# Sinkhorn attention and a Sinkhorn-routed mixture on one core: the last sums of expert 0's first weights are put behind VectorE's sums of x, and a weight fetch in front of them

## The chip, the core and the metric

The kernel runs on one core of a Trainium2 chip. The metric is the device time of one execution, in microseconds (us). The core has five engines with queues of their own, which meet only through semaphores: TensorE (PE, matrix multiply; its weight loads are listed as PEld), VectorE (DVE), ScalarE (ACT), GpSimd (POOL) and SyncE (SP, here only for transfers). Matmuls write to PSUM, which is used here as 8 banks of 128 x 512 float32; everything else lies in SBUF. Transfers run beside the engines, but each is issued by an instruction on the queue of SP, ACT or POOL.

## The reference

Two stages in a row: block-sorted attention, whose output is the x of a mixture of experts with Sinkhorn-balanced gates.

```python
# attention: batch 4, heads 8, sequence 768, head size 64, 8 blocks of 96
P = sort_net                                   # 8 x 8 for each batch and head
for _ in range(5):                             # exp, then rows and columns to sum 1
    P = np.exp(P - P.max(-1, keepdims=True))
    P = P / (P.sum(-1, keepdims=True) + 1e-09)
    P = P / (P.sum(-2, keepdims=True) + 1e-09)
k_sorted = einsum('bhij,bhjcd->bhicd', P, k_b) # blocks of k and v mixed by P
v_sorted = einsum('bhij,bhjcd->bhicd', P, v_b)
attn = softmax(scale * q_b @ k_sorted.T)       # within each block
x = (attn @ v_sorted) as 3072 tokens x 512
# mixture: 8 experts, 512 -> 1024 -> 512
P = np.exp(x @ w_gate - max)
for _ in range(8):                             # rows, columns, times N / E
    P /= P.sum(1, keepdims=True) + 1e-09; P /= P.sum(0, keepdims=True) + 1e-09; P *= N / E
for e in range(8):
    out += P[:, e:e+1] * (np.maximum(x @ w1[e], 0) @ w2[e])
```

## The kernel before

**Two parts.** The first part goes through the four batches of attention. While batch bb is at work, PE also gets pieces of expert 0's dense work on the tokens of batch bb - 1 (`expert0`), so that it has something to do while ACT and DVE prepare the next scores. The second part works off the rest of expert 0 (tokens 2048 to 3071) and experts 1 to 7, with seven block products in place of eight (a Strassen-like scheme): it needs sums and differences of blocks of w1 (`sum_w`), of x (`sum_x`), of w2 (`sum_w2`) and of the hidden layer.

**Who sets the order.** `pin` keeps an instruction at its place in the written order of its engine; what is not pinned is placed by a scheduler. All work of PE and POOL in the stretch concerned is pinned but for one memset; the first `sum_x` on DVE is not. Attention of batch bb follows a string, `PLANS[bb]`: q, k, s, d, m are queries, keys, scores, sums and mixing for a pair of heads, a number n takes n pieces of expert 0's work, g and l are gate logits, L loads the next batch, v sorts values. W and w in `PLANS[3]` take 9 and 2 sums from `w1_sums`, a chain of `sum_w(1)` and `sum_w(0)`, eight sums for each expert, all on POOL (L323). `load_next(3)` took five before. So of the sixteen, five come with the load, nine at W (the last three of expert 1 and six of expert 0), two at w. For expert 0 the two that overwrite blocks of w1 itself come last (`late`).

**PSUM in the first part.** Scores, sums, mixing and expert 0 share a ring of 8 banks (pool `pa`): a matmul into a bank waits until the bank's reader of eight allocations ago is done. The matmuls of L221 (scores) are 16 for a pair of heads, into four banks, eight matmuls for two banks at a time. The matmuls of L408 fill a bank with an output tile of expert 0, which L413 copies to SBUF on DVE or ACT. L395 is the hidden layer of expert 0, L262 mixes the values, L265 scales the result into `xtT` (x transposed) on DVE, L253 and L254 on ACT form the reciprocal of the softmax sums that L244 has formed.

**Around the seam.** After attention `load_w2(1)` fetches expert 1's w2 into a new pool, on POOL's queue (L95). `onesc` is a memset on POOL (L556). `sum_x(0, nc.vector, ...)` makes four sums on DVE (L552), over the first of three token ranges: three into `xc`, one that overwrites a block of `xtT`. `xs` is `sum_x(2, nc.vector)`, the third range; `sum_x(1, nc.gpsimd)` is the second, on POOL. `held_x` is a copy of two columns of `xc` (L807) that keeps POOL waiting for the third of `xs`'s sums; behind it stand the eight sums of w2 (L542). The sums of expert 0's w1 lie in `osbl`, in tiles that the output doesn't need yet; PE reads them at L611.

```python
    3: "1 g q0,q1,k0,k1,k2 3 q2,q3,s0 W 4 k3,d0,s1 4 m0,d1,s2 6 m1,d2,s3 4 w 1 m2,d3 2 m3 1"
    ...
    w1_sums = in_turn(sum_w(1), sum_w(0))
    ...
    for a, b, c in ((b12, b11, x1), (b22, x1, x2), (b21, x2, x4), (b22, b12, b12)):
        hold(eng.tensor_tensor(out=c, in0=a, in1=b, op=ALU.subtract))
```

Of the kernel before, what the change touches and what calls it, by code (L numbers as in the profile page):

```python
# [15 lines left out]
BF16 = mybir.dt.bfloat16  # L16
# [10 lines left out]
def kernel(  # L27
# [11 lines left out]
    nc = tc.nc  # L39
# [20 lines left out]
    pin = tc.keep_in_program_order  # L60
# [3 lines left out]
    xtT = xtp.tile([128, 4, N], BF16)  # L64
# [79 lines left out]
    def sort_values(bb, bank, n=8, h0=0):  # L144
        for h in range(h0, n):
            vps = bank([128, 384], F32)
            pin(nc.tensor.matmul(vps, Rt[bb][:, h].rearrange("p i c -> p (i c)"),  # L147
                                 vt[bb][:, h, :], start=True, stop=True))
            (nc.vector.tensor_copy if bb == 0 and h in (3, 5, 7) or bb and h % 2 else
             nc.scalar.copy)(  # L150
                vs[:, :, h, :], vps.rearrange("p (kk d) -> p kk d", d=64))
            if h % 2:
                yield

        for i in (0, 1, 2, 3, 4, 6, 5, 7) if bb == 0 else range(NB if n == 8 else 0):
            eng = ((nc.scalar if i == 1 else nc.gpsimd if i in (5, 7) else nc.sync)
                   if bb == 0 else nc.gpsimd if i % 2 and bb == 1 else nc.sync)
            if bb == 0 and i == 5:
                yield
            (pin if bb == 0 else lambda ins: ins)(eng.dma_start(  # L160
                out=mkap(vsbt[bb % 2], [[VW, 96], [1, 512]], off=i * 512),
                in_=vs[16 * i:16 * i + 16].rearrange("p kk h d -> p kk (h d)")))
# [3 lines left out]
    def queries(bb, hp, bank):  # L166

        qps = bank([128, 6, 128], BF16)
        if bb < 2:

            for kk in range(6):
                for h in range(2):
                    pin(nc.tensor.matmul(qps[64 * h:64 * h + 64, kk, :],
                                         qt[bb][:, 2 * hp + h, kk * 64:kk * 64 + 64],
                                         Ibig, is_transpose=True, start=True, stop=True))
        else:
            qr = sp.tile([128, 6, 2, 64], BF16, name="qr", bufs=2)
            nc.gpsimd.tensor_copy(
                qr.rearrange("p kk h d -> p h kk d"),
                qt[bb][:, 2 * hp:2 * hp + 2].rearrange("p h (kk d) -> p h kk d", d=64))  # L180
            for kk in range(6):
                pin(nc.tensor.matmul(qps[:, kk, :], qr[:, kk].rearrange("p h d -> p (h d)"),  # L182
                                     Ibig, is_transpose=True, start=True, stop=True))
        qT[bb, hp] = sp.tile([128, 128, 6], BF16, name="qTs", bufs=4)
        (pin if bb == 0 else lambda ins: ins)(
            (nc.scalar.copy if bb == 0 or hp < 2 or bb == 1 else nc.vector.tensor_copy)(
                qT[bb, hp], qps.rearrange("p kk c -> p c kk")))

    def keys(bb, hp, bank):

        kT[bb, hp] = sp.tile([128, NB, 16, 6], BF16, name="kTs", bufs=4)
        for b in range(2):
            kps = bank([128, 3, 128], F32)
            for j in range(3):
                kk = 3 * b + j
                for h in range(2):
                    pin(nc.tensor.matmul(  # L197
                        kps[64 * h:64 * h + 64, j, :],
                        kt[bb][:, 2 * hp + h, kk * 64:kk * 64 + 64],
                        Rt[bb][:, 2 * hp + h].rearrange("p i c -> p (i c)"),  # L200
                        start=True, stop=True))
            (order if bb == 0 else lambda ins: ins)(
                (nc.scalar.copy if (bb, hp, b) in ((0, 0, 1), (0, 1, 0)) else nc.vector.tensor_copy)(
                    kT[bb, hp][:, :, :, 3 * b:3 * b + 3],
                    kps.rearrange("p kk (i c) -> p i c kk", i=8)))
# [65 lines left out]
    def logits(bb, bank, ks):  # L271

        if 0 in ks:
            gp[bb] = bank([128, TB, E], F32)
        for kk in ks:
            for t in range(TB):
                c = bb * S + t * 128
                pin(nc.tensor.matmul(gp[bb][:, t, :], xtT[:, kk, c:c + 128], wg[:, kk],
                                     start=(kk == 0 and t == 0), stop=(kk == 3),
                                     skip_group_check=True))  # L280
        if 3 in ks:
            nc.vector.tensor_copy(glog[:, bb * TB:(bb + 1) * TB, :], gp[bb])

    def first_attention(bank, warm, fill):
# [9 lines left out]
        for x in PLAN0.split():  # L294
# [8 lines left out]

    wct = {}

    def sum_w(e):

        if e:
            wct[e] = (wcq if e % 2 == 0 else wcp).tile([128, 3, 2, F // 2], BF16, name="wc")
        else:  # L310
            wct[e] = osbl[:, NT - 3:].rearrange("p t d -> p (t d)").bitcast(BF16).rearrange(
                "p (j k f) -> p j k f", j=3, k=2)
        late = []
        for kk in range(2):
            a11, a21 = (w1t[e][:, kk, f:f + 512] for f in (0, 512))
            a12, a22 = (w1t[e][:, 2 + kk, f:f + 512] for f in (0, 512))
            s1, s2, s4 = (wct[e][:, j, kk, :] for j in range(3))
            todo = [(a21, a22, ALU.add, s1), (s1, a11, ALU.subtract, s2),
                    (a11, a21, ALU.subtract, a21), (a12, s2, ALU.subtract, s4)]
            if e == 0:  # L320
                late.append(todo.pop(2))
            for a, b, o, c in todo + (late if e == 0 and kk else []):
                pin(nc.gpsimd.tensor_tensor(out=c, in0=a, in1=b, op=o))  # L323
                yield
# [11 lines left out]
    w1_sums = in_turn(sum_w(1), sum_w(0))  # L336

    def attention(bb, bank, fill):

        def sorts():  # L340
            for b in {1: (1, 2), 2: (3,), 3: ()}[bb]:
                yield from sort_values(b, bank)
                yield

        values = sorts()

        def step(what, hp):
            if what == "q":
                queries(bb, hp, bank)
            elif what == "k":  # L350
                keys(bb, hp, bank)
            elif what == "s":
                scores(bb, hp, bank)
            elif what == "l":
                logits(bb, bank, (0, 1, 2))
            else:
                for b in range(2):
                    (sums if what == "d" else mix)(bb, hp, b, bank)

        for x in PLANS[bb].split():  # L360
            if x == "v":
                next(values)
            elif x == "g":
                logits(bb - 1, bank, (0, 1, 2, 3))
            elif x == "L":
                load_next(bb + 1)
            elif x in "Ww":
                for _ in range(9 if x == "W" else 2):
                    next(w1_sums)
            elif x.isdigit():  # L370
                for _ in range(int(x)):
                    next(fill)
            else:
                for y in x.split(","):
                    step(y[0], int(y[1]))
# [132 lines left out]
    mpc, xcp, wq, wcq = late("mpc", 1), late("xcp", 1), late("wq", 2), late("wcq", 1)  # L508
# [36 lines left out]
    xc = xcp.tile([128, 3, 2, N // 2], BF16)  # L545

    def sum_x(p, eng, hold=pin):
        ta, tb = (slice(1024 * p + 512 * i, 1024 * p + 512 * i + 512) for i in range(2))
        b11, b12, b21, b22 = (xtT[:, k:k + 2, t] for k in (0, 2) for t in (ta, tb))
        x1, x2, x4 = (xc[:, j, :, 512 * p:512 * p + 512] for j in range(3))  # L550
        for a, b, c in ((b12, b11, x1), (b22, x1, x2), (b21, x2, x4), (b22, b12, b12)):
            hold(eng.tensor_tensor(out=c, in0=a, in1=b, op=ALU.subtract))  # L552
            yield

    onesc = mpc.tile([128, 128], F32)
    nc.gpsimd.memset(onesc, 1.0)  # L556
    for _ in sum_x(0, nc.vector, lambda ins: ins):
        pass

    def balance():  # L560
# [230 lines left out]
    for i in (0, 2):  # L791
        take = iter(six[i]).__next__
        two = [hidden(0, 2, i + j, hTb[1], None, False, take)[0] for j in range(2)]
        for n, step in enumerate([f for both in zip(*two) for f in both]):
# [8 lines left out]
            if (i, n) == (0, 5):  # L803
                for _ in xs:
                    pass
    held_x = mpc.tile([128, 2], BF16)
    pin(nc.gpsimd.tensor_copy(held_x, xc[:, 2, 0, 1024:1026]))  # L807

    queue = [sum_w2(1), sum_x(1, nc.gpsimd)]

# [13 lines left out]
    for m, o in enumerate(ends):  # L824
        e, p, hT, _ = chunks[-1]
# [4 lines left out]
    for r in range(len(pairs) + 6):  # L830
        n, i = r // 4, r % 4
        if n < C:
            e, p, hT, s3 = chunks[n]
# [83 lines left out]
```

## Time and profile before

| | |
|---|---|
| Runs before, median (lowest to highest of 3) | 662.59 us (662.49 to 663.95) |
| The profiled execution, whole | 662.44 us |
| Its span in the profile | 660.7 us |
| Granted clock of PE over the span | 1.0 |
| Chain that ended last, share of PE | 95% |
| Of it L611 and L724, the second part's matmuls | 40% and 38% |
| POOL's wait for expert 1's w2 and two later ones, L542 (3 times) | 15.5 us |
| POOL's wait for PE's L395, at L323 | 8.5 us |
| POOL's wait for DVE's sum of x, at L807 | 3.5 us |

Times in a timeline are counted from the start of the span. In such a row the first number is the start, the second the duration, and brackets hold how long the engine sat idle before it, and what ended that. Where a row says x2 or more, the duration covers all of them. The profiled execution has the instructions' durations; it is one of the kernel's runs, and its own time stands beside its span so that sums over rows are made against it.

### The profile page before, as it was taken

To read this page: it belongs to the slowest core of one execution; us is meant where nothing else is said; L and a number is where in the kernel's file an instruction comes from. 1 tells how busy PE (TensorE), PEld (TensorE's weight loads), DVE (VectorE), ACT (ScalarE), POOL (GpSimd) and SP (SyncE) were. 2 spreads that over 40 slices of the span, in tenths; PEclk is the share of its full clock that TensorE was granted. 3 is DMA by queue.
4 is the path that set the end of the run, shared out by engine and by line. 5 is a ranking of instruction groups with operands and counts; after the bars stand their busy time and mean duration, and the time that the engine had idled before them with its cause. 6 is when DMAs were issued, how large, how long until landed. Compare 5 with 4: busy or idle time off the path is not lost.

```text
span 660.7 us, 13144 instructions
## 1 busy us (share of the span) xinstructions
PE 647.5 (98%) x5035; PEld 422.0 (64%) x5035; DVE 476.2 (72%) x897; ACT 390.1 (59%) x765; POOL 476.2 (72%) x438
## 2 busy tenths in 40 slices
PE   5999998999999999999999999999999999999997
PEld 2556665445666666666666666666666666666665
DVE  6857587666777777777777777777777777777775
ACT  5877766757777755555555555555555555555540
POOL 3543564477999898689696969799796969946641
PEclk9999999999999999999999999999999999999999
DMA  9999930406103040211303040302103040000224
GB/s 150 183 222 143 204 64 1 65 1 97 32 1 64 2 65 1 44 22 15 50 1 65 1 65 1 65 1 38 27 3 63 1 64 2 1 1 34 95 80 176
DMA packets 34031, 36.52 MB, mean 55 GB/s; under 512 B 2352, under 2 KB 27376, under 8 KB 33968
## 3 DMA queue, kind: packets, MB, share of 16 engines
q0 software_dynamic: 26448, 26.81, 26.1%
q1 hardware_dynamic: 7120, 8.38, 4.4%
q8 instruction: 39, 0.64, 0.4%
q10 hardware_dynamic: 400, 0.49, 0.2%
q14 instruction: 24, 0.20, 0.1%
HBM read 52.45 MB, written 6.29 MB: 89 GB/s over the span
## 4 chain that ended last, share of the span: by engine, by line
PE 95%; DMA 2%; DVE 1%; issue 1%; POOL 1%; DVEq 0%; POOLq 0%
PE bk L611 40%; PE oacc L724 38%; PE bank L395 4%; PE bank L408 4%; PE oacc L778 2%; DMA kt<-in_k_dram 2%; PE bank L221 1%; PE bk L690 1%; PE bank L262 1%; PE bank L244 1%; PE bank L197 1%; PE bank L147 1%; PE oacc L611 1%; PE bank L182 0%; DVE xc L552 0%
## 5 line engine op out<-in xcount | busy, mean ns | idle before, releaser
L674 DVE SCALAR_TENSOR_TENSOR osbl<-oacc,glog,osbl 128x256 f32<-128x256 f32 (+1 forms) x411 | 219.2, 534 | 125.6 <-PE oacc L724 117.6
L597 ACT ACTIVATE hT<-bk 128x512 bf16<-128x512 f32 x173 | 103.2, 598 | 143.3 <-PE bk L611 135.7
L611 PE MATMUL bk<-xtT,w1e 128*128 128x512 bf16 x518 | 152.6, 379 | 0.0
L724 PEld LDWEIGHTS <-hs 128*128 128x128 bf16 x984 | 96.3, 98 | 62.8
L724 PEld LDWEIGHTS <-hT 128*128 128x128 bf16 x904 | 88.4, 98 | 57.7 <-issue 0.3
L714 POOL TENSOR_TENSOR hs<-hT 128x512 bf16<-128x512 bf16 x82 | 94.9, 1157 | 37.4 <-DVE hT L600 32.1
L724 PE MATMUL oacc<-w2e,hT 128*128 128x256 bf16 x764 | 114.6, 273 | 0.1
L714 POOL TENSOR_TENSOR hs<-hs,hT 128x512 bf16<-128x512 bf16 x82 | 94.8, 1156 | 6.4
L714 POOL TENSOR_TENSOR hs<-hT,hs 128x512 bf16<-128x512 bf16 x82 | 94.7, 1155 | 6.4
L611 PE MATMUL bk<-xc,wc 128*128 128x512 bf16 x336 | 99.1, 379 | 0.0
L724 PE MATMUL oacc<-w2e,hs 128*128 128x256 bf16 x616 | 92.4, 273 | 0.0
L611 PEld LDWEIGHTS <-w1e 128*128 128x128 bf16 x704 | 68.8, 98 | 14.9 <-issue 0.5
L648 ACT COPY p<-bk 128x512 f32<-128x512 f32 x84 | 49.3, 586 | 25.7 <-PE bk L611 25.7
L600 DVE CUSTOM_DVE_ANT_0 hT<-bk,p 128x512 bf16<-128x512 f32 x84 | 58.1, 691 | 7.8 <-PE bk L611 3.4
L642 ACT COPY u<-bk 128x512 f32<-128x512 f32 x84 | 49.3, 587 | 22.5 <-PE bk L611 22.2
L633 ACT COPY bk<-bk 128x512 f32<-128x512 f32 x85 | 48.6, 572 | 20.3 <-PE bk L611 20.3
L600 DVE CUSTOM_DVE_ANT_0 hT<-bk,u 128x512 bf16<-128x512 f32 x84 | 57.0, 679 | 1.8 <-PE oacc L589 1.2
L724 PE MATMUL oacc<-w2s,hs 128*128 128x256 bf16 x368 | 55.2, 273 | 0.0
L611 PEld LDWEIGHTS <-wc 128*128 128x128 bf16 x504 | 49.3, 98 | 8.7 <-issue 0.2
L667 DVE SCALAR_TENSOR_TENSOR s<-bk,hT 128x512 bf16<-128x512 f32 x80 | 54.4, 680 | 0.0
L611 PE MATMUL bk<-xc,w1e 128*128 128x512 bf16 x172 | 51.0, 379 | 0.0
L611 PE MATMUL bk<-xtT,wc 128*128 128x512 bf16 x168 | 50.0, 379 | 0.0
(145 smaller groups left out, 836.9 us busy)
## 6 DMA issues: line engine op xcount, KB each, us to landing
w2e<-in_moe_w_dram POOLq DMA_DIRECT2D x8, 1024.0 KB, 9.8
w1e<-in_moe_w_dram POOLq DMA_DIRECT2D x7, 1024.0 KB, 9.0
out_dram<-osbl SPq DMA_DIRECT2D x21, 256.0 KB, 2.0
vsb<-vs SPq DMA_DIRECT2D x25, 96.0 KB, 3.8
vt<-in_v_dram POOLq DMA_DIRECT2D x3, 768.0 KB, 12.3
qt<-in_q_dram POOLq DMA_DIRECT2D x4, 384.0 KB, 10.5
kt<-in_k_dram POOLq DMA_DIRECT2D x4, 384.0 KB, 12.3
kt<-in_k_dram POOLq DMA_DIRECT2D x2, 768.0 KB, 14.2
```

The lines of the kernel that those rows point to most:

```text
L395: pin(nc.tensor.matmul(hps[:, 0:n], w1t[0][:, kk, fb * 128:(fb + 1) * 128], xtT[:, kk, c0:c0 + n], start=(kk == 0), stop=(kk == 3)))
L408: pin(nc.tensor.matmul(oacc, hTs[:, fb, tt * 128:(tt + 1) * 128], w2t[0][:, fb, :], start=(fb == 0), stop=(fb == 7)))
L597: relu = lambda o, x: nc.scalar.activation(out=o, in_=x, func=AF.Relu)
L600: return nc.vector._custom_dve(TENSOR_ADD_SAT, out=o, in0=x, in1=y, s0=TOP, s1=0.0)
L611: pin(nc.tensor.matmul(ps, wa[:, kk, :], xa[:, kk, :], start=(first and kk == 0), stop=(kk == 1), skip_group_check=True))
L633: pin(nc.scalar.copy(t["w"], t["u"]))
L642: pin(nc.scalar.copy(t["u2"], t["u"]))
L648: pin(nc.scalar.copy(t["p5"], t["v"]))
L667: pin(nc.vector.scalar_tensor_tensor(out=s3[:, i, :], in0=t["w"], scalar=0.0, in1=c12, op0=ALU.max, op1=ALU.subtract))
L674: pin(nc.vector.scalar_tensor_tensor(out=o, in0=ps, scalar=glog[:, t, e:e + 1], in1=o, op0=ALU.mult, op1=ALU.add))
L714: pin(nc.gpsimd.tensor_tensor(out=s[:, c], in0=a, in1=b, op=o))
L724: pin(nc.tensor.matmul(ps, h[:, fb, :], w[:, fb, :], start=(first and fb == 0), stop=(fb == 3), skip_group_check=True))
```

## The change

POOL's order around the seam is changed. `PLANS[3]` has no w any more (its place becomes part of a 5), and W takes six sums: the last three of expert 1 and the first three of expert 0. The remaining five of expert 0 are taken after DVE's `sum_x(0)`, and in front of them stand, in this order: the fetch of expert 1's w2 (its place in the code is the same, the sums have moved past it), the memset of `onesc` (now pinned), a copy of two columns of `xc` that DVE's third sum writes, and a copy of two columns of `xtT` that its fourth writes. The three copies share a tile `held`; the one that was `held_x` is its third part. What is computed is the same.

```diff
-             3: "1 g q0,q1,k0,k1,k2 3 q2,q3,s0 W 4 k3,d0,s1 4 m0,d1,s2 6 m1,d2,s3 4 w 1 m2,d3 "
-                "2 m3 1"}
+             3: "1 g q0,q1,k0,k1,k2 3 q2,q3,s0 W 4 k3,d0,s1 4 m0,d1,s2 6 m1,d2,s3 5 m2,d3 2 m3 1"}
...
-            elif x in "Ww":
-                for _ in range(9 if x == "W" else 2):
+            elif x == "W":
+                for _ in range(6):
                     next(w1_sums)
...
     onesc = mpc.tile([128, 128], F32)
-    nc.gpsimd.memset(onesc, 1.0)
+    pin(nc.gpsimd.memset(onesc, 1.0))
     for _ in sum_x(0, nc.vector, lambda ins: ins):
+        pass
+    held = mpc.tile([128, 3, 2], BF16)
+    for j, a in enumerate((xc[:, 2, 0, 0:2], xtT[:, 0, 512:514])):
+        pin(nc.gpsimd.tensor_copy(held[:, j], a))
+    for _ in w1_sums:
         pass
...
-    held_x = mpc.tile([128, 2], BF16)
-    pin(nc.gpsimd.tensor_copy(held_x, xc[:, 2, 0, 1024:1026]))
+    pin(nc.gpsimd.tensor_copy(held[:, 2], xc[:, 2, 0, 1024:1026]))
```

POOL's queue in the stretch, as the two programs have it (line numbers of before):

| before | after |
|---|---|
| L323, first three sums of expert 0 | L323, first three sums of expert 0 |
| L323, next three | L95, fetch of expert 1's w2 |
| L556, memset | L556, memset |
| L323, last two (wait for L395) | copy of `xc`, waits for DVE's last L552 of the first range |
| L95, fetch of expert 1's w2 | copy of `xtT` |
| L807, held copy | L323, next three sums |
| L542, eight sums of w2 | L323, last two (wait for L395) |
| | L807, held copy |
| | L542, eight sums of w2 |

## The prediction

> **What bounds the kernel now.** I read the page's engine table first, then PE's own list of waits, then the timeline of the 10 us in which the one large wait lies, engine by engine.
>
> ```profile
> PE 647.5 (98%) x5035; PEld 422.0 (64%) x5035; DVE 476.2 (72%) x897; ACT 390.1 (59%) x765; POOL 476.2 (72%) x438
> PE bank L173 <- DMA qt<-in_q_dram: 6.8, 1, 6.8
> PE bank L221 <- DVE osbl L413: 2.0, 2, 1.6
> PE bank L466 <- DVE Prep L458: 0.2, 1, 0.2
> ```
>
> TensorE (PE) is busy for 98% of the span. It waits for something a listed 9 us in all: 6.8 us for the first q, before any work can start, and 2.0 us at L221 (scores of attention), for VectorE's (DVE's) copy of expert 0's output out of PSUM at L413. Only the second lies near the change. PE around it (start, duration, and in brackets the idle time before):
>
> ```profile
> 98.10 0.56 PE L221 MATMUL bank<-qTs,kTs 64*96 64x96 bf16 x16
> 98.59 3.63 PE L408 MATMUL bank<-w2e,hTs 128*128 128x512 bf16 x16
> ...
> 102.94 0.38 PE L221 MATMUL bank<-qTs,kTs 64*96 64x96 bf16 x8
> 104.90 0.20 PE L221 MATMUL bank<-qTs,kTs 64*96 64x96 bf16 x1 [1.58 <-DVE osbl L413]
> 105.50 0.34 PE L221 MATMUL bank<-qTs,kTs 64*96 64x96 bf16 x7 [0.40 <-DVE osbl L413]
> 105.77 1.90 PE L408 MATMUL bank<-w2e,hTs 128*128 128x512 bf16 x8
> ```
>
> One head pair's scores are 16 such matmuls. Undisturbed, the next work starts 98.59 - 98.10 = 0.49 us after them; at 102.94 it starts 105.77 - 102.94 = 2.83 us after. So the wait costs 2.34 us from start to start (the 1.58 + 0.40 of the brackets leave out time in which PE counts as busy draining). The second eight matmuls need the two PSUM banks that the L408 of 98.59 filled, and DVE empties them late:
>
> ```profile
> 98.86 0.71 DVE L552 TENSOR_TENSOR xc<-xtT 128x1024 bf16<-128x1024 bf16 x1
> 99.60 1.53 DVE L552 TENSOR_TENSOR xc<-xtT,xc 128x1024 bf16<-128x1024 bf16 x1
> 101.05 1.63 DVE L552 TENSOR_TENSOR xtT<-xtT 128x1024 bf16<-128x1024 bf16 x1
> 102.61 1.64 DVE L552 TENSOR_TENSOR xc<-xtT,xc 128x1024 bf16<-128x1024 bf16 x1
> 104.17 1.27 DVE L413 COPY osbl<-bank 128x512 f32<-128x512 f32 x2
> ...
> 117.51 1.42 DVE L552 TENSOR_TENSOR xc<-xtT,xc 128x1024 bf16<-128x1024 bf16 x2
> ```
>
> The same sum takes 0.71 us at 117.51 and up to 1.64 us here. What runs on GpSimd (POOL) tells the two places apart:
>
> ```profile
> 97.86 1.16 POOL L323 TENSOR_TENSOR osbl<-w1e,osbl 128x512 bf16<-128x512 bf16 x1
> 98.98 1.60 POOL L323 TENSOR_TENSOR osbl<-w1e 128x512 bf16<-128x512 bf16 x1
> 100.66 1.48 POOL L323 TENSOR_TENSOR osbl<-osbl,w1e 128x512 bf16<-128x512 bf16 x1
> 102.22 1.48 POOL L323 TENSOR_TENSOR osbl<-w1e,osbl 128x512 bf16<-128x512 bf16 x1
> ```
>
> POOL's three sums grow from 1.16 to 1.48 to 1.60 us over exactly the stretch in which DVE's grow; at 117.51 POOL is idle. The two hold each other up, one for one. POOL's sums at 94.28 to 97.86 keep 1.15 to 1.16 us while DVE copies out of PSUM (L186, L203), so it is the sums on both sides, not any two instructions, that collide.
>
> **The change part by part.** By the built program, PE, DVE and ACT keep their order and their waits; only POOL's queue differs.
>
> *Three sums leave the stretch.* The three POOL sums of 98.98 (second half of expert 0's w1) now stand behind a copy that waits for DVE's fourth sum. DVE's first sum starts at 98.86 as before and still meets the tail of POOL's 97.86 sum, so 0.71 us stands. The other three follow at 0.71 us each: 99.60 + 3 x 0.71 = 101.73, where DVE is done at 104.17 now: 2.4 us earlier. The L413 copies take 1.27 / 2 = 0.64 us each: the first from 101.73 to 102.37, the second (its matmuls end at 98.59 + 3.63 = 102.22, so it need not wait) to 103.01. PE wants both banks after its first eight matmuls, at 102.94 + 0.49 / 2 = 103.19. Margin 0.18 us: the wait goes whole, -2.34 us.
>
> *What is late next.* L408 at 103.43 needs the bank that ACT's L253 reads: it starts at 102.91, 0.87 us for two, so 0.44 each, done at 103.35. The L395 matmuls behind it need banks from DVE's L265 (1.01 us for two, from 103.01, so free at 103.5 and 104.0, wanted at 105.2 and later) and from ACT's exponentials, which run on from 104.50 at 0.43 us each and are done at 106.2; the last is wanted by L244 at 109.71 - 2.34 = 107.37. All hold, the first by under 0.1 us. From 105.8 on all engines wait for PE or for each other, so the rest of the kernel shifts whole. I take 0 to 0.1 us for the tight ones, 0.04 as the value.
>
> *The sums themselves.* The copies cost 0.18 us each (the row of the one held copy now). POOL: DVE done at 101.73, two copies to about 102.15, three sums started 1.24 us apart (as 95.39, 96.63, 97.86 do now): done at 105.9 instead of 103.70. Queued behind them are two w1e sums that wait for PE's last L395 (112.30 now, 109.96 then), so nothing there is late; PE first reads these sums at 118.76 - 2.34 = 116.4. Cost 0, with 4 us of cover.
>
> *The fetch and the memset in front.* Expert 1's w2 is issued at 99.02 instead of 114.50 (0.95 us on POOL). By the program it waits for the last L197 matmul of attention (over at 97.85) and for loads long landed, so it does not hold up POOL. The DMA queues are empty from 97 us until now's fetch at 114.5, so it meets no transfer. It lands about 9.4 us later (114.50 to 123.94 now), at 108.5. While it is issued, and during the 0.21 us memset, DVE's second and third sums run; the trace shows no such sum beside an issue. From below it costs 0; from above DVE stops for 0.95 + 0.21 = 1.16 us, of which 0.18 is margin: 0.98 us. [...]
> [...]
>
> *After the fetch.* The eight w2 sums of POOL start behind the held copy (119.00 - 2.34 = 116.66), at about 116.9, instead of waiting for the fetch until 123.94. So the first of them meets DVE's last sum for the third token range (119.74 - 2.34 = 117.40), which takes up to 1.64 instead of 0.68 us, 0.96 us more. PE reads its result at 121.35; now it is done at 120.42, so 0.93 us are free. Cost 0 to 0.03 us. POOL's own gain of 4.7 us goes nowhere: its L664 at 137.61 waits for DVE's hT again.
> [...] Alone, 0.71 + 1.16 = 1.87 us a pair; the pairs here start 102.22 - 100.66 = 1.56 us apart, so the measured rows say it is less. [...]
>
> **Sum.** -2.34 + 0.04 = -2.30 us. The profiled execution took 662.44 us (span 660.7, 1.7 us around it): 660.14. The median of the runs, 662.59, is 0.15 above it: 660.3 us.
>
> **Rivals.**
> *The issue or the memset stops DVE.* Bounds as above: 0.2 to 0.98 us of the 2.30 are lost, 660.5 to 661.3, say 660.9. For it: POOL and DVE do collide here. Against: neither row reads two tiles as the sums do. 15%.
> *DVE's sums are slow for another reason* (the first use of xc, say), and stay so. Then PE waits as now: 662.6. Against: at 98.98 to 103.7 POOL's rows stretch too, and nothing but DVE's sums is there to stretch them. 10%. That the change doesn't do what it says is the same case: POOL's three sums still within DVE's.
> *POOL goes first at 116.9.* If DVE's last sum is not let in after one POOL sum but after all eight back to back (8 x 1.16 = 9.3 us), it ends near 126.2 + 0.7 = 126.9; PE's reader of 121.35 - 2.34 = 119.0 stands, 7.9 us, net +5.6: 668.2. It is slower than before once DVE waits for three sums or more (3 x 1.16 - 0.93 = 2.55 > 2.30). Against: between 98.98 and 104.25 the two alternate one for one, and the second w2 sum waits for the first, which leaves a gap. 7%.
>
> **How the numbers follow.** The forecast has 68%: 659.9 to 660.7 by itself (gains of 1.9 to 2.7). A measurement of this kernel tells about 0.3%, 2.0 us, from no change, so 660.6 parts faster from same: the forecast lies 0.3 us beyond it. Nine tenths of it fall below, with a little of the first rival: faster 0.63. Same: the rest of the forecast, most of the first rival and all of the second: 0.30. Slower: 0.07. For 8 in 10 the range runs from 659.6 to 662.6.
>
> **What would show it.** Right: L552 on DVE at 0.7 us four times from 98.86; no bracket at PE's L221; L408 near 103.4 instead of 105.77; POOL's L323 at 1.16 us from 102.2; the fetch issued at 99.0. Wrong: an L552 above 1 us beside the issue (first rival), a PE wait at L611 near 119 (third), or a new wait of PE anywhere after 105 us that takes back what L221 gave.

## The result, and the profile after

| | before | changed |
|---|---|---|
| Median (lowest to highest, 8 runs each) | 662.98 us (662.19 to 664.85) | 660.41 us (660.12 to 662.22) |
| Ratio, with its 95% interval | | 0.9959 [0.9945, 0.9973] |
| The profiled execution, whole, and its span | 662.44, 660.7 us | 660.12, 658.3 us |

The kernel became 2.6 us faster. Line numbers move by a little: L413 of before is L412 here, L408 is L407, L395 is L394, L552 is L551, L323 is L322, L611 is L615. PE's waits in the changed kernel (us in total, times, longest):

```profile
PE bank L173 <- DMA qt<-in_q_dram: 6.4, 1, 6.4
PE bank L465 <- DVE Prep L457: 1.6, 1, 1.6
```

The wait at L221 for DVE's copy out of PSUM, 2.0 us before, is no longer listed. These two lie in the first 13 us; the only others are four waits of 0.16 to 0.31 us at L407 and L147, all before 88 us. PE's timeline in the stretch (start, duration):

```profile
102.53 0.49 PE L244 MATMUL bank<-atp,one 96*64 96x384 bf16 x4
102.95 0.56 PE L221 MATMUL bank<-qTs,kTs 64*96 64x96 bf16 x16
103.46 1.89 PE L407 MATMUL bank<-w2e,hTs 128*128 128x512 bf16 x7
...
116.44 1.89 PE L615 MATMUL bk<-xc,osbl 128*128 128x512 bf16 x8
```

All 16 score matmuls go in one piece, and the next work starts 0.51 us after them where it started 2.83 us after. The matmuls that read expert 0's sums start at 116.44 instead of 118.76: the 2.32 us won at L221 are still there 13 us later. DVE's timeline, and POOL's:

```profile
98.87 0.70 DVE L551 TENSOR_TENSOR xc<-xtT 128x1024 bf16<-128x1024 bf16 x1
99.60 0.69 DVE L551 TENSOR_TENSOR xc<-xtT,xc 128x1024 bf16<-128x1024 bf16 x1
100.21 0.69 DVE L551 TENSOR_TENSOR xtT<-xtT 128x1024 bf16<-128x1024 bf16 x1
100.81 0.69 DVE L551 TENSOR_TENSOR xc<-xtT,xc 128x1024 bf16<-128x1024 bf16 x1
101.41 0.69 DVE L412 COPY osbl<-bank 128x512 f32<-128x512 f32 x1
102.27 0.69 DVE L412 COPY osbl<-bank 128x512 f32<-128x512 f32 x1 [0.17 <-PE bank L407]
...
117.42 1.09 DVE L551 TENSOR_TENSOR xtT<-xtT 128x1024 bf16<-128x1024 bf16 x1
```

```profile
98.96 0.95 POOL L95 DMA_DIRECT2D w2e<-in_moe_w_dram  x1
99.90 0.23 POOL L555 MEMSET onesc<- 128x128 f32 x1
101.56 0.18 POOL L560 COPY held<-xc 128x2 bf16<-128x2 bf16 x1 [1.44 <-DVE xc L551]
...
101.83 1.15 POOL L322 TENSOR_TENSOR osbl<-w1e 128x512 bf16<-128x512 bf16 x1
...
116.81 1.15 POOL L541 TENSOR_TENSOR w2s<-w2e 128x512 bf16<-128x512 bf16 x1
118.05 1.48 POOL L541 TENSOR_TENSOR w2s<-w2e,w2s 128x512 bf16<-128x512 bf16 x1
```

Four sums of x at 0.7 us, where three took 1.53 to 1.64; the first copy out of PSUM starts at 101.41 instead of 104.17, and the second even waits 0.17 us for PE, so DVE is no longer late at all. In the built order DVE's sum over `xtT` comes third and the last one into `xc` fourth, so POOL's copy of `xc` does the waiting and the copy of `xtT` follows it at once. POOL's sums are back at 1.15 us behind the held copies. The issue of the fetch and the memset run beside DVE's sums and don't lengthen them (0.69 us each, from 99.60 to 101.50). At 117.42 the collision that the early w2 sums bring is seen: 1.09 instead of 0.68 us on DVE, 1.48 instead of 1.15 on POOL.

### The profile page after: what moved, and what is told of

Same layout as the page of the kernel before. It is cut to its first block, busy times and chain, and to the rows that moved or that the text cites. A ratio compares the mean times of both kernels' runs of the same rounds, so it can differ in the third digit from the quotient of the medians.

```text
span 658.3 us, 13067 instructions
## 1 busy us (share of the span) xinstructions
PE 641.6 (97%) x4956; PEld 421.4 (64%) x5035; DVE 474.2 (72%) x897; ACT 389.6 (59%) x765; POOL 475.4 (72%) x440
## 4 chain that ended last, share of the span: by engine, by line
PE 89%; POOL 6%; issue 1%; ACT 1%; DVE 0%; DVEq 0%; ACTq 0%; POOLq 0%
PE oacc L728 35%; PE bk L615 35%; PE bank L407 4%; PE bank L394 4%; POOL hs L718 4%; PE oacc L782 2%; PE bank L221 1%; PE bank L262 1%; POOL wc L322 1%; PE bk L694 1%; PE bank L244 1%; PE bank L197 1%; PE bank L147 1%; PE oacc L615 0%; PE bank L182 0%
## 5 line engine op out<-in xcount | busy, mean ns | idle before, releaser
L615 PE MATMUL bk<-xtT,w1e 128*128 128x512 bf16 x491 | 146.9, 379 | 1.0
L615 PE MATMUL bk<-xc,wc 128*128 128x512 bf16 x319 | 95.5, 379 | 0.1
L615 PEld LDWEIGHTS <-w1e 128*128 128x128 bf16 x704 | 68.8, 98 | 15.0 <-issue 0.5
L615 PEld LDWEIGHTS <-wc 128*128 128x128 bf16 x504 | 49.3, 98 | 8.7 <-issue 0.2
L615 PE MATMUL bk<-xc,w1e 128*128 128x512 bf16 x161 | 48.8, 379 | 0.1
L615 PE MATMUL bk<-xtT,wc 128*128 128x512 bf16 x159 | 48.0, 379 | 0.5
```

Source lines behind the costliest of these rows:

```text
L615: pin(nc.tensor.matmul(ps, wa[:, kk, :], xa[:, kk, :], start=(first and kk == 0), stop=(kk == 1), skip_group_check=True))
```

## The experiments

Theory A: the gain is DVE's four sums at 0.7 us. Theory B: it is the early fetch. The measure is taken from the timeline of each profile: from the start of the 16 score matmuls at L221 to the start of the expert's matmuls behind them, 0.51 us in the changed kernel and 2.83 in the one before. It came out alike on other chips: 0.51 in the changed kernel again, 2.85 in before_again and before_b.

| run | POOL's sums beside DVE's | L221 to L407, us | median, us | ratio to before [95%] |
|---|---|---|---|---|
| changed, again | 0 | 0.51 | 660.45 | 0.9942 [0.9925, 0.9959] |
| hold_only | 0 | 0.51 | 660.54 | 0.9940 [0.9923, 0.9958] |
| hold_last | 0 | 0.52 | 660.75 | 0.9942 [0.9924, 0.9960] |
| dve_later | 0, DVE has two sums more | 1.01 | 661.03 | 0.9947 [0.9930, 0.9964] |
| hold_7 | 1 | 0.91 | 661.45 | 0.9963 [0.9948, 0.9979] |
| hold_8 | 2 | 1.87 | 661.92 | 0.9968 [0.9955, 0.9982] |
| fetch_only | 3 | 3.37 | 665.05 | 1.0005 [0.9992, 1.0018] |

The runs hold_only, fetch_only, dve_later and hold_last are from one chip, the changed kernel again, hold_7 and hold_8 from another; the kernel before took 664.54 us on the first and 664.25 on the second. The ratios are to these.

**hold_only: the copies without the fetch in front.**

```diff
-    load_w2(1)
...
     for _ in w1_sums:
         pass
+    load_w2(1)
```

> The two copies and the five sums as in the changed kernel, but the fetch of expert 1's w2 back behind the five sums. Theory A (the gain is VectorE's four sums at 0.7 instead of up to 1.64 us, so that the L412 copies free the two banks in time): PE's wait at L221 stays away, L407 after the scores starts near 103.4 as in the changed kernel, GpSimd waits for w2 at its first w2 sum until about 121 us again; ratio to the kernel before 0.9960 to 0.9970, that is 2.0 to 2.6 us less. Theory B (the fetch in front brings the gain, as GpSimd is done with the w2 sums 4.7 us earlier): the time of before, ratio 1.000.

The L407 matmuls start at 103.31, 0.51 us after the scores; DVE's sums take 0.69 to 0.71 us; the time is 660.54 us. Theory A holds. The saving against before is larger than expected, 4.0 us, and that is taken up under the clock below. The fetch in front makes no difference that the medians show (660.41 and 660.45 with it, on other chips), but without it the profile has a wait of PE that neither the changed kernel nor the one before has:

```profile
122.00 0.27 DVE L581 TENSOR_REDUCE gm<-gmr 1x1 f32<-1x128 f32 x1 [1.00 <-DMA gmr<-gm]
122.92 1.02 PE L614 MATMUL bk<-xc,osbl 128*128 128x512 bf16 x4 [0.42 <-DVE hT L603]
```

A transfer of 0.5 KB for the gates (`gmr<-gm`) lands 4.8 us after its issue here, where the fetch is in flight, and after 2.0 us in the changed kernel, where the fetch is over. In the nine profiles with the late fetch it takes 4.1 to 4.8 us, in the five with the early one 2.0. DVE waits for it, so its part of the hidden layer (L603) is late, and PE waits for that. The fetch in front is thus no part of the 2.3 us at L221, but it keeps a wait of 0.4 us from taking its place.

**fetch_only: the fetch in front, nothing held.**

```diff
-    pin(nc.gpsimd.memset(onesc, 1.0))
+    for _ in w1_sums:
+        pass
+    pin(nc.gpsimd.memset(onesc, 1.0))
...
-    for j, a in enumerate((xc[:, 2, 0, 0:2], xtT[:, 0, 512:514])):
-        pin(nc.gpsimd.tensor_copy(held[:, j], a))
-    for _ in w1_sums:
-        pass
```

> The fetch in front of the five sums as in the changed kernel, but without the two copies, so that nothing makes the sums wait; the memset stands behind them. The issue moves the first of GpSimd's sums from 98.98 to 99.92. Theory A: VectorE's second sum then also runs alone, the third and fourth still collide at 1.5 to 1.6 us; L412 starts near 103.2 (before 104.17, changed 101.41), L407 near 104.8, so 0.9 to 1.0 us less than before, ratio 0.9985. Theory B: the whole gain, ratio 0.996.

Both numbers were wrong: there is no gain at all. Its timeline on DVE, and on POOL (this execution runs 3.4 us later):

```profile
102.27 0.73 DVE L551 TENSOR_TENSOR xc<-xtT 128x1024 bf16<-128x1024 bf16 x1
103.03 2.05 DVE L551 TENSOR_TENSOR xc<-xtT,xc 128x1024 bf16<-128x1024 bf16 x1
105.01 1.64 DVE L551 TENSOR_TENSOR xtT<-xtT 128x1024 bf16<-128x1024 bf16 x1
106.57 1.64 DVE L551 TENSOR_TENSOR xc<-xtT,xc 128x1024 bf16<-128x1024 bf16 x1
```

```profile
102.39 0.95 POOL L95 DMA_DIRECT2D w2e<-in_moe_w_dram  x1
103.36 1.17 POOL L322 TENSOR_TENSOR osbl<-w1e 128x512 bf16<-128x512 bf16 x1
```

The second sum was expected to run alone. It had started 0.33 us before POOL's sum, and yet it lost more than the whole length of that: it ends 0.55 us after POOL's, at 105.08, having taken 2.05 us, 1.36 more than alone. POOL's sum lost nothing. With three collisions instead of the two expected, the wait became 0.54 us longer than before (3.37 against 2.83), as much as the median (665.05 against 664.54). So theory B falls: by the timeline the fetch alone makes the stretch longer, and by the times (ratio 1.0005) it gains nothing.

**dve_later: no collision, but a later VectorE.**

```diff
+        more = [(b12, b11, xc[:, j, :, 1024:1536]) for j in range(0 if p else 2)]
-        for a, b, c in ((b12, b11, x1), (b22, x1, x2), (b21, x2, x4), (b22, b12, b12)):
+        for a, b, c in (*more, (b12, b11, x1), (b22, x1, x2), (b21, x2, x4), (b22, b12, b12)):
```

> The changed kernel with two more sums of x on VectorE (the first one again, into columns of xc that are overwritten later), GpSimd held back as before. The built order puts two of six sums between the two L412 copies. Theory A: sums of 0.6 us each from start to start put the second L412 at 103.2 to 103.9, where PE wants its bank at 103.2: a wait of about 0.7 us at L221 comes back with no collision at all, and the time is 0.7 us over the changed kernel's, ratio to before 0.9970 to 0.9975. If the lateness of VectorE is not what PE waits for: no change, ratio as the changed kernel's.

The second L412 runs from 103.15 to 103.83, and L407 starts 1.01 us after the scores, 0.50 us more than in the changed kernel: the scores take 0.85 us instead of 0.56, and L407 has a wait of 0.16 us for L412. The median is 0.3 us above hold_last's on the same chip, and 0.6 above the changed kernel's on the others. So a late DVE brings a wait back with no collision, in the size of its lateness. The expected 0.7 was too much by 0.2. The two added sums also change what this kernel computes, though the columns that they write are written again later; why stays open, and only its times are used here.

**hold_last: no late collision.**

```diff
     pin(nc.gpsimd.tensor_copy(held[:, 2], xc[:, 2, 0, 1024:1026]))
+    pin(nc.gpsimd.tensor_copy(held[:, 3], xtT[:, 0, 2560:2562]))
```

> The changed kernel with one more held copy, which makes GpSimd's w2 sums wait for VectorE's last sum over the third token range as well; that sum took 1.09 us at 117.42 in the changed kernel against 0.68 before. Theory A: the sum falls back to 0.7 us, the second w2 sum from 1.48 to 1.16 us, and the time stays within 0.1 us of the changed kernel's, since PE reads the result only at 119.03. Rival: the collision delays the gate chain on VectorE and costs up to 0.4 us, which this run wins back.

The sum takes 0.68 us again (at 118.26), and the time doesn't fall: 660.75 us, against 660.41 and 660.45 for the changed kernel on other chips. The profiles agree: from the first matmul that reads expert 0's sums to the end of the span there are 541.9 us here (659.2 - 117.29) and in the changed kernel (658.3 - 116.44). The late collision is covered; the rival's 0.4 us is not there.

**The changed kernel again, hold_7, hold_8: one, two or no collision.** In hold_7 and hold_8 only the number at W differs from hold_only.

```diff
             elif x == "W":
-                for _ in range(6):
+                for _ in range(7):      # hold_8: 8
```

> The changed kernel once more, on the chip of the next two. Theory A with a second part that the last runs suggest (the wait at L221 in the kernel before also lowers the granted clock behind it in part of the executions, to 0.997 over the span, and each of those costs 1 to 1.5 us more): granted clock 1.00 over the span in all executions here; the kernel before has 0.997 in those of its executions that take over 664 us and 1.00 in the others; the gain is 2.3 us against the latter and 3.5 to 4 against the former. Rival: the kernel before is slower on that chip for a reason outside the stretch, and its clock does not sort its times.

> The two copies hold back only two of the three sums (the fetch stands behind them, as in hold_only); one sum collides. Theory A: VectorE's second sum takes 1.53 us, the others 0.7; the L412 copies start 0.85 us later than in the changed kernel, near 102.25; PE's second bank comes 0.35 us late, so L407 starts at 103.8 to 103.9; 0.4 us over the changed kernel, granted clock 1.00.

> The two copies hold back one of the three sums; two collide. Theory A: L412 starts near 103.2, L407 near 104.8, 1.35 us over the changed kernel. If the clock falls behind any wait: 0.997 and another 1 to 1.5 us; if only behind the longer wait of the kernel before: 1.00 and no more than the 1.35.

The steps come as expected in the timeline: 0.91 us (0.40 over the changed kernel's 0.51) and 1.87 us (1.36 over). DVE's rows in hold_8 show the count directly, two long sums and two short ones:

```profile
98.97 0.72 DVE L549 TENSOR_TENSOR xc<-xtT 128x1024 bf16<-128x1024 bf16 x1
99.72 1.53 DVE L549 TENSOR_TENSOR xc<-xtT,xc 128x1024 bf16<-128x1024 bf16 x1
101.17 1.64 DVE L549 TENSOR_TENSOR xtT<-xtT 128x1024 bf16<-128x1024 bf16 x1
102.73 0.68 DVE L549 TENSOR_TENSOR xc<-xtT,xc 128x1024 bf16<-128x1024 bf16 x1
```

Both have the fetch behind the sums, as hold_only has, and with it the second wait of PE at L614: 0.44 us in hold_7, 0.16 in hold_8. The median of hold_8 is 1.47 us over the changed kernel's (1.36 + 0.16 = 1.52). That of hold_7 is 1.00 over where 0.4 was expected; the second wait, which was not thought of, makes it 0.40 + 0.44 = 0.84. Two of hold_7's twelve executions took over 664 us, which its profile doesn't explain.

**copies, memsets: what of POOL's work holds DVE up.** Both are the kernel before with the three colliding sums replaced, by two copies or four memsets each.

```diff
+                if e == 0 and kk and n < 3:
+                    for _ in range(2):                     # memsets: range(4)
+                        pin(nc.gpsimd.tensor_copy(c, b))   # memsets: nc.gpsimd.memset(c, 0.0)
+                else:
+                    pin(nc.gpsimd.tensor_tensor(out=c, in0=a, in1=b, op=o))
```

> The kernel before with each of the three colliding sums replaced by two copies of one input (so the second half of expert 0's sums is left out of the result). It asks what of GpSimd's work holds VectorE up. If any reading of SBUF by GpSimd does: VectorE's second to fourth sums take over 1 us again and PE waits at L221. If only sums of two inputs do: 0.7 us each and no wait at L221.

> The kernel before with each of the three colliding sums replaced by four memsets of the same tile (so the second half of expert 0's sums is left out of the result). GpSimd then writes in that stretch, and reads nothing. If it is GpSimd's reading that holds VectorE up (the copies of one input took VectorE's sums to 0.98 and 1.09 us): 0.7 us each and no wait at L221. If its writing does too: over 0.9 us.

DVE's second to fourth sums beside the copies (L551 is L556 here), and the third beside the memsets, where all three take 0.68 or 0.69 us:

```profile
100.09 0.98 DVE L556 TENSOR_TENSOR xc<-xtT,xc 128x1024 bf16<-128x1024 bf16 x1
100.99 1.09 DVE L556 TENSOR_TENSOR xtT<-xtT 128x1024 bf16<-128x1024 bf16 x1
102.00 1.09 DVE L556 TENSOR_TENSOR xc<-xtT,xc 128x1024 bf16<-128x1024 bf16 x1
```

```profile
100.55 0.68 DVE L556 TENSOR_TENSOR xtT<-xtT 128x1024 bf16<-128x1024 bf16 x1
```

What POOL reads is what counted here: DVE's sums took 0.3 to 0.4 us more beside copies of one input, 0.84 to 0.95 beside sums of two, nothing beside memsets, though POOL was at them without a break from 99.29 to 104.8. From the scores to the expert's matmuls it takes 1.21 us with the copies and 0.52 with the memsets; each ran once, in 661.28 and 660.48 us.

**before_again, before_b, before_c: where the clock is low.** The kernel before, unchanged, one profile each.

> The kernel before once more, for a profile of an execution whose clock is not 1.00 over the span, if this is one (26 of 36 were). Theory A, second part: the granted clock is low in one stretch of 5 to 7 us that begins behind PE's wait at L221, as it was 0.74 from 109.6 to 116.2 behind the longer wait of fetch_only, and 1.00 before and after; the matmuls in it take up to 1.5 times as long, 1.5 to 2 us in all. Rival: the low clock lies elsewhere, in the first 40 us say, and the wait at L221 costs its 2.34 us alone.

> The kernel before, a second time for its profile (the first had a granted clock of 1.00 throughout, and 662.9 us). If this execution's clock is 0.997 over the span: Theory A, second part, has it low only in 5 to 7 us behind PE's wait at L221; the rival has it low elsewhere, as it was in fetch_only once more between 20 and 40 us. If it is 1.00: near 662.7 us, and where the low stretch lies in the kernel before stays argued from the counts.

The third had the second's expectation. All three have a clock of 0.999 to 1.00 and 662.75 to 662.97 us, so no profile of the kernel before shows a low clock. What there is: of the 41 executions of it whose clock was recorded, the 13 at 0.999 or above have a median of 662.97 us (662.22 to 663.94), the 28 at 0.997 or below 664.70 (663.81 to 667.83). None of the 24 executions of the changed kernel (again), hold_only, hold_last and dve_later, and none of hold_8's 8, is that low; 11 of fetch_only's 12 are, and 2 of hold_7's 12. The profile of fetch_only shows two low stretches. The one behind the wait at L221 (in each row the stretch, its length, the busy time of PE, PEld, DVE, ACT and POOL with their instructions, then the granted clock, the share of the DMA engines and GB/s):

```profile
core 0: us, PE busy (x) PEld busy (x) DVE busy (x) ACT busy (x) POOL busy (x), PEclk, DMA share, GB/s
108.00:110.00 2.00, 0.74 (x9) 0.48 (x10) 2.00 (x5) 0.95 (x4) 0.00 (x0) 1.00 1.19 191
110.00:112.00 2.00, 1.95 (x7) 0.81 (x7) 0.34 (x1) 0.69 (x2) 0.00 (x0) 0.66 0.27 47
112.00:114.00 2.00, 2.00 (x11) 1.25 (x9) 0.69 (x1) 0.38 (x1) 0.00 (x0) 0.50 0.00 0
114.00:116.00 2.00, 2.00 (x39) 1.41 (x39) 1.33 (x4) 0.66 (x2) 0.00 (x0) 0.98 0.00 0
```

With the 0.50 of the third row as the low clock, these rows hold 1.36 + 2.00 + 0.08 = 3.44 us of it, and the cost is half of that, 1.72 us. That is the difference between the two medians of the kernel before (664.70 - 662.97 = 1.73), and 1.72 of 661 us is the 0.003 by which the mean clock falls. The other low stretch of that profile follows a wait of 1.91 us at L262 for a transfer, at 28 us, and sums to 3.44 us as well (clock 0.68, 0.50 and 0.96 from 28 to 34 us, two us each). So in this execution a wait of PE may have cost twice: its own length, and the stretch at half clock behind it. It need not: the four profiles of the kernel before all have a wait of about 1.6 + 0.4 us at L221, and no low clock. Nor need L221 be the only source, for hold_7 has two executions at 0.997, and in its profile only 0.22 us of wait there. That the low clock of the kernel before lies behind L221 is argued from the counts, not shown. Why only some executions are hit, no run here shows.

## Why the prediction was right

The forecast of 660.3 us met 660.41, and 660.14 for the profiled execution met 660.12. The interval of the ratio is 0.14% to either side, so the gain of 0.4% is clear of noise; the prediction had counted with 0.3%.

- *What bounds the kernel.* Right: the 2.34 us at L221 became 2.32 us of gain, and hold_7, hold_8 and dve_later put parts of it back in the sizes of DVE's lateness.
- *Three sums leave the stretch.* Right in the mechanism. Done at 101.50 instead of the 101.73 worked out: sums that don't need the one before follow after 0.60 us, not 0.71. So the second copy did have to wait, 0.17 us for its L407, and the margin was set by PE and not by DVE.
- *What is late next.* Right: no wait of PE between 103 and 117 us in the timeline after.
- *The sums themselves.* Right: they end at 105.44 (105.9 expected), and the two behind them at 109.98 still wait for L394, 4.53 us.
- *The fetch and the memset.* The sum counts 0 for their cost, the low end of 0 to 0.98 us; no row of before shows that. It came true: the sums beside them took 0.69 us. The fetch landed 9.1 us after its issue (9.4 expected), so DVE's sums didn't hold it up either. The first rival falls here. In fetch_only the sum that began under the issue was held up, but by POOL's sum.
- *After the fetch.* Right in the cost: the meeting cost DVE 0.41 us (up to 0.96 allowed), covered, as hold_last shows. POOL's head start is gone at its L668, which waits 4.68 us for DVE's hT. It left out the gates' small transfer: a fetch that stays late meets it, and hold_only pays 0.42 us for that.
- *Rivals.* The second falls with copies and memsets: only POOL's work was changed in those, and DVE's sums changed with it. The third falls with the row at 117.42: DVE was let in after one sum.
- *What it didn't have.* The clock. The profiled execution of before had 1.00 throughout and so showed nothing of it. The sum was made against that execution and fits it (662.44 - 660.12 = 2.32); the medians differ by 2.57. On the chips of the experiments, where most executions of the kernel before were hit, the change is worth 3.8 us (660.45 against 664.25), of which the sum accounts for 2.3. Against the 13 executions at full clock it is 2.5.

## What to carry to other kernels

When one instruction shape takes two durations in a trace, look at what the other engines read at the time: DVE's sum took 0.68 us beside POOL's memsets and up to 1.64 beside its sums of two inputs. If the longer one stands ahead of a copy that frees a PSUM bank, moving the other engine's work by a few us may be worth the whole wait, 2.32 us here. To make POOL's queue wait for an event on DVE, a copy of two columns of the tile was enough: 0.18 us. When a large fetch can go earlier, look for small transfers that it would meet where it stands: the one of 0.5 KB took 4.3 us in the kernel before and 2.0 in the changed one. Behind waits of PE of 1.91 and of 2.12 + 0.40 us the profile of fetch_only shows stretches at half clock, and the four of the kernel before, with about 1.6 + 0.4 us, show none, so compare the granted clock of several executions, and not of the profiled one alone.

## What the hardware showed that was not expected

- A DVE sum that had started 0.33 us before POOL's still lost more than the whole of it (2.05 us, fetch_only), while at 98.98 in the kernel before, a POOL sum that started 0.12 us after DVE's lost 0.44 us to it. Who goes first is not settled by the recorded starts; why the two differ stays open.
- Sums that collide don't run wholly one after the other by the recorded times: they take 0.69 and 1.16 us alone, 0.60 and 1.11 from start to start, and run in pairs 1.56 us apart.
- The clock: about 3.44 us at half clock, 1.72 us of time, behind waits of 1.91 and of 2.12 + 0.40 us in one execution; in none of hold_8's 8, with a wait of 0.63 + 0.40 us.
- A transfer of 0.5 KB took 4.1 to 4.8 us beside a fetch of 1 MB (4.3 in the kernel before, 4.8 in hold_only), and 2.0 us without one (the changed kernel).
